# One order of work for five engines, searched again: 1789 operations re-listed, 39 of them on another engine

## The chip, the cores and the metric

The kernel runs on one core of a Trainium2 chip. Five engines work there at the same time, each through its own list of instructions in order: TensorE (PE, matrix products; loading its weights is shown as PEld), VectorE (DVE), ScalarE (ACT), GpSimd (POOL) and SyncE (SP). SP, ACT and POOL also issue DMA transfers. An instruction that needs another engine's result waits at the head of its engine's list, and all that stands behind it on that engine waits too. The metric is the device time of one execution in microseconds; before the change the median of three runs is 204.81 us.

## The reference

Two stages follow each other. The first is block-sparse attention for 4 batches, 8 heads, 768 positions and 64 values per head. Keys and queries are cut in blocks of 32; a query block sees its neighbours, the first and the last block, and three drawn blocks; the first and last query blocks see everything.

```python
scores = scale * np.matmul(q, k.transpose(0, 1, 3, 2))
scores = np.where(mask, scores, -1000000000.0)
scores = scores - np.max(scores, axis=-1, keepdims=True)
attn = np.exp(scores)
attn = attn / (np.sum(attn, axis=-1, keepdims=True) + 1e-09)
return np.matmul(attn, v).astype(np.float32)
```

The heads of one position are put side by side (512 values), and the second stage is a feed-forward net with a gate: a product with `w_in` (512 to 1024), relu, a convolution over three neighbouring positions in each of the 1024 features, a sigmoid of it, and a product with `w_out`.

```python
h = np.maximum(x @ w_in, 0.0)
for k in range(K):
    conv_out += conv_w[k][None, None, :] * hp[:, k:k + S, :]
gate = 1.0 / (1.0 + np.exp(-conv_out))
return (h * gate @ w_out).astype(np.float32)
```

## The kernel before

**The pieces of attention.** Two heads make a pair P, so there are 16 pairs, four for each batch. A pair's keys and queries come in by two ways. Pairs 0 to 4 (`kq_transposes`, line 426) are loaded, transposed by PE (`k_tr`, `q_tr`, lines 470 and 508) and copied by DVE or ACT into a slot (`k_cp`, `q_cp`). Pairs 5 to 15 (`kq_crossbar`, line 546) are loaded by POOL, transposed by a DMA that SP issues (`xb`, line 585) and copied by DVE (`stg_cp`, line 592). The mask sits in 24 extra rows of the same tiles, so that a score product adds it; these rows are made on the first microseconds by DVE and ACT (lines 267 to 363). Values are loaded by POOL and copied (`v_cp`, line 622).

**The unit.** The scores are worked off in 144 units of 128 x 1024 numbers (loop at line 724). A unit is two groups of score products on PE (`s`, line 746), one `exp` on ACT (line 757) from one of two PSUM tiles `st` into one of eight SBUF tiles `pt`, and two groups of four products with the values (`av`, line 779). Since there are two `st` tiles, the scores of unit u+2 wait for the exp of unit u. In this document exps and units are counted from 0, in the order in which they are made.

**The feed-forward part.** The positions are cut in nine segments (line 668): seven of 384 positions, one of 256, one of 128. When the four pairs of a segment are through, DVE divides by the row sums (`rcp`, `norm`, lines 696 and 698), the features are turned by a DMA on SP (`x_xb`, line 707) or by PE with a copy behind it (`x_tr`, `x_cp`, lines 717 and 720), and PE multiplies by `w_in` (`f1`, line 895). Relu (line 903) is an operation of ACT or DVE. For most of the work the convolution is three multiplications and two additions on DVE (`mul`, `add`, lines 946 and 956), then a tanh on ACT (line 998), one more addition and the gate's product on DVE (`g1`, `g2`, lines 1001 and 1006). The last segment's convolution is done on PE (`conv`, line 970). PE multiplies by `w_out` (`f2`, line 825, and line 810 for the last 128 rows), ACT or DVE copies the sum out of PSUM (`ev`), and SP or ACT writes it (`out`).

**What sets the order.** The kernel makes 1789 operation objects and doesn't issue them as it makes them. `put_down` (line 95) walks through the text `ORDER` (line 20) and issues them one by one. Two characters number an operation; where it can run on two engines a letter follows (`A` for ACT, `V` for DVE), and where it takes a buffer a character gives the buffer's number. So the text holds the order of every engine's list, the engine of each operation with a choice, and each buffer. The times given to `op` (`{"DVE": 0.6}`, `lat`, `earliest`, `service`, the priorities) and the lists `deps` and `uses` were read by the search that wrote the text; `put_down` reads none of them. The waits between engines come from the tile framework, which sees which tile each instruction reads and writes.

**The gates of the loads.** POOL issues the loads of K, Q and V in one list. From pair 8 on a `pace` stands ahead of a load (lines 415 to 420): POOL copies one number out of the `pt` tile of a chosen unit, so it waits for that unit's exp. `PACE_U` (line 422) gives the units.

**What is told to be apart.** `apart` (line 868) declares that the relus of the segment of 256 positions and the multiplications and gates of the segment ahead of it touch other columns of the feature tile `hE`, so that the framework puts no wait between them.

Of the kernel before, what the change touches and what calls it, by code (L numbers as in the profile page):

```python
# [20 lines left out]
000x010z020B0407080905060b1e00a1f1c01q11s11801m11t1E21G21H030y0e0c0gV0d0nV0f0A0i0hA0WA30UA0oAr41r5r6r7r8r9rarb  # L21
rcrdrerfrgrhrirjrkrlrmrnrorprqrrrsrtrurvrwrx0Y01210ZA014A0VA13A0mA0XV0jV0+V0lV0t0uryrzrArBrCrDrErFrGrHrIrJrK
15017A16ArLrM4n04o0/14s14t1g11j04p00q10V0p11V1hV11lV1kV4u11dV01iV4x04yrN0rOrPrQ4C14D4z2rRrSrTrUrVrWrXrY4H04I
4E34J44q14r4v4w4Q14R4S54A4B4F4G0s0r1rV14V04W4K1u04X64+14/5071x11vV21yV1zV4L0530544T4U4Y4Z5c15d510E15505e10C1wV
4M01FV24N0F0k5h05i1I0525j21JV35m15n5o31L1561NV575811MV5r05s5f15g5w15x1KV1911n00I5t45y55F05G1bV591S30O0P0Q0R46
1A0470S481O1490T4a1U44b1V4c2404d2634e271TV34f2c14g2e04h2f4i2k24j2m11aV1oV0N1pV5H65k5l5p5q5K15L5M75u5v5z5P05Q
5A05I4O15R05U15V5W15J5a05N610625O5S5T5X5Y6324PV00J5bV5B20D5C5Z35+661675D15EV6416b06c5/0651B160V0K1DV1CV6836d4
0w0v6g16hhq0hr6i56l06m6n6ht1hu6t16uhsV0hvVhO0hQhP6v7hI0hJ6y06zhw1hxhKA6A0hyVhRhS6D16E69hz0hA6F16a1P16e6f6j6I0
6k6J6ohBA1QVhW11RVhT6q0hX6r6K26Q1hF06RhGhC1hD6S3hEAhHVhU6V06W6+11W06p06/6X47056w6x6B73074hL1hM781756hNA796C6G
7a77g06H6L6M6T17h6U6Y1Z17i07l17m6Z717276777q07r7b7n1hYhZi221XV41YVi3i4h+hV06N1i5ia36O1+Vh/ib7d21/V25V4i0ic7ei6  # L30
7s27v17w7c0ii07jio17kid7D07E7x37o7p7t7u7y7z7F4i76s1280292g12h6P7f7I17J7N07G17H7O7A37K5i17P67Biei8i92aV02bVifig
ih2dV02iV17Cijip7S17Tiq7X07Lik7U77Y7M7Q7R831847Vir7Z0851880897Wil8d18e7+8a22jVisV04k2n4l2s34mimV18002lV12tV281
iu18i08j8f38k4ix0iyizV8q18riviwViS4iTiUiV8v08wiA0iBiD1iE8s58x6iCAiFAi+0iW2o22p2qV22rV2u2002v22x2w8A18B7/08F086
878GiG08b8c8g8hiJ1iH8C78H0iXiIA8l8m8t18K18L8S08T8uiK2108yj08n1i/8oj122ViLV23Vj61j28M18U28z8X18Y8D8E8I8J90091
8Z3925j38N8O08ViM1951iP0969769d08WiQiNiOA8+9e8/939i194989j998P2j7iYj8j4iZj98Qj59a3iRVja9bje29f79k1jfjgjhji9n0
9o9p3jE1jbjs09g19s19t9u69h9l9x09yjt9z79mjF9F19q9r9G9v9w9A9K09L9B0jcjdjGjujj9H19M62F2G42C2D02Q2I2H2N2O12R32T2S
2Y2Z22y08222z2J18p8R9c9P19Q9R4jkjljHjIV29C02AV39Djv9I9U09Va019Ja1jN1jOjwA39W0a22jK0jLjMA1jPV0Gk63a50a6aa1jQ19N
abjT0jRk7k8jSVk9jUa75ac3jVA2/30032312Kaf0agak1alah7jZ1j+am1j/A9O9SjW09T9X9Yas0a31ata4a8jXa9ax1ayk31k4ke4kakb0L
kg9Z10H2BVjYVkm0knkf2LV4au6az4aC0aDaE0k00adk1aH1aeaIk2AaiajanaP0aQaJ2jm0jnkh9+ki2MVap2k5Vkcku1aU1aVaR5aW3kjjo
aZ0a+jpao0avawb21b3jy1aAaBaFaGaKaLa/7aqkv2EV32PV4kpkd1kob70b8kqkxaM3kk2+V0aNkwkl9E32U22Vin330jxarit349/b46jqA4  # L40
jzbf1bgb94jAjBbk0kI0aS1blaTaXaYaObh0krbm2jCA1bp1b0bqb1b5kJbu0bvb6ksky2WV02XVktbr5kzkAkBkC1babb0kD373833a3b13f
3c3d3ebw13mbC1bDbc035V1kEkKbH0kFbE3bIbM1bNkLkGV339A1bdkMV036VkO1kPbibJ7bO6kQVbR0bSkR0kSbT4kTVla2lblcldlebW1bj
bXbnbobsbY0kX1c20c3btkU0c71c8c42c95kYkVbxbykWAkZVbz2bAli3cc0cdbF1bGch1cibKl11ce1lfbLl2cp0cj3cqk+0bPbQbUbVbZb+0
cu1ljlklll3Vlmb/1lgc0cr7lnlhloc5l71cvk/l0Alq4cz0c6cacbcfcgcAcw6l40lplrlsltl5l8ckcE1clcFcm3l9VlucB0l6Aly0lzcnlB
lAlC3p3n03q23u3r3s3tcG4cJ0cKcs1ctcxcycClM0cL2lvcR1lG1cDcScW0cT5cHcXcY3cIlNcMcN0lHcUcVc/1d0d40d5lDjDbe03g13hjJ
c1bB3v23wcokHd17lwlxd66cZlIc+lOdc1ddde43iV2lElFd2lP3jVlQV1lJdh0lKA2didj5dm1dnm20m3d3do73E3B3F43J3G3xV3m4V0cO0
cPme1mfmgV3yVdr0d7dsm50m6dw1d8dxdt1m7Vmq1mrmsmtmud913oV23H3T3U33C13Idy03Y3V3W3Q3R23X43443df1mb1dE0dFdG2m80m9mc
dJ1mdAmaAdadKdgdO0dPdL6dQ3mh1mk0mlmidkdT1dUdldpdqdudvmjAd/0e0dzmn1dV4e41e5dA0dHdImoe15e67mpAe90eaeb1mvmy2mmVmz
mG3mImHmJmKmAdB2mBdCmCmO4lS0dMdNdRee1dSefdWdXlTe21e3lY1eg0mLdY3mwmx0mPlUej0eklZl+lVe7l/mDmQdZmRmMmS3DV3mEel2
m0A3e8er1esecew0edehexet6kN3kjr3K03LlR3Z1cQ1lWA0mFn01eieB1eCemn1mN3MV4mTey3eD4mUmV3NVeo0epmW0mXen0mYmZeG0eH  # L50
m+A4n2n3db3+3/V03zlLdDn4V140V3SV4eO1eP3Pd+nf0m1423leq2lX3O3An5ngnc1nd45A0eI5eQ7neAnhVnC0eT0eUeY1eZn90nan61n7
eV1e+0nEnDnbVn8AnFnu1f10f2euevf61f7nl0ezf32nmni1fe0f86nvnGnwnHnxnnVffeAnjeEnkVfj1fkeFeJeKfg3fl4nynzeL1nK2nLeM
nMnIeR1eSeWeXfo0fpno0e/f0ft1fuf4f5fq5f9nr1nsfv7fa0fB0fCnpfhfG1fHfifmfnfrfsfwfxfb2nNnAnJnqVnBntAfcnOfy3nS3fD1
fI0fL0fMfzn+1fN2fT1fUfE1fFo40nTnUnVnWfY0fJfZfKnPfV641eNfdfAf+3nXnQfOn/o5nRg11g2fPfQ0fW0fXf/g90g0g34gao0o6gb5g4
ge1gffRnYnZo7o1o2V2o8A3gg7gj0gkg5om0ong610MooA1gl1op1oqgc1gr1g7orVoK4oMoLoNoOov0gsgt0os1gdowoxAgw0otouAgxgB1gh
gCgioB0gmgnoCgy2oS0go2oDVgpfS3g8o9gqgD6oPgK0oy1ozgLgP1oH0oIgQgu0oAAgM3oE1gvgzgAgEoFgX0gYgR4oJAoGAoToUo+1o/p0p1
oVgFh31gN1gZ5gG3oQgHoWoXog0gOgSohgU0p62h4gI1h80h9gT0oiojp7oYp8oR1p9gVgJApap2h57okA0pq1prhh1g+pz0g/h61pApsApC3
h01ha1pBApbp3oa1h7hbobocodh1pEpDpFhd2pcpdp4oZpt0puhioeA1pvAgW0h2m/hep5pK4pLpw1pxhj0pyAhc0pk0plpmhf1pnhkhlpGpN
p+2p/hm3hnpMq1hgApoA3pHpOpS0pTpIpUpVpJpWpe1pfpgho0phhpApiA4ql0qmqnAqo1qpqi0qz1qAqjpPqqAqB1qkApppjolo3ofqE0qF
qr1qsqu1qvpQqCpRq60q7qDq0pXqtAqw3qG4qxq2q3qypYpZqc1qJ1qKqdqO0qL1qeqHq4qMq5q8q9qNqIqaA3qfqPqQqRqgA4qbqhqSA0qTS  # L60
qU0qVqWqXq+1qYA2qZSq/r0r1r2Ar3A
# [52 lines left out]
def kernel(  # L114
# [118 lines left out]
    o_pad = op("pad_mem", {"DVE": 0.4}, pad, -18, after=[o_amem])  # L233
# [4 lines left out]
    def dma(name, eng, dst, src, prio, deps=(), service=0.3, kind="hw", **kw):  # L238
        occ = {"SP": 0.46, "ACT": 0.1, "POOL": SW}[eng]
        return op(name, {eng: occ}, lambda e: on(e).dma_start(out=dst(), in_=src), prio, deps,  # L240
                  dma=(kind, service), **kw)

    qf, kf = o2s_t[0], [o2s_t[1], o2s_t[2]]
    def first_q(x, e, prio, after):
        return dma("ld_q0", e, lambda: qf[:, 192 * x:192 * x + 192],
                   q[0, x, 0:384].rearrange("(p c) d -> p (c d)", p=128), prio, service=0.38, earliest=1.0, after=after)

    def first_k(x, e, prio, after):
        return dma("ld_k0", e, lambda: kf[x][:, 0:384], k[0, x].rearrange("(p c) d -> p (c d)", p=128), prio,
                   service=0.75, earliest=1.0, after=after)  # L250
# [4 lines left out]
    ld_sb = op("ld_sb", {"SP": 0.46}, lambda e: nc.sync.dma_start(out=sbi, in_=sampled_blocks.bitcast(I32)), -21,  # L255
               after=[k0], lat=1.8)
# [813 lines left out]
```

## Time and profile before

| what | before |
|---|---|
| median of three runs (lowest, highest) | 204.81 us (204.47, 206.22) |
| span of the profiled execution | 202.8 us |
| busy: PE, PEld | 196.8 us (97%), 153.9 us (76%) |
| busy: ACT, DVE, POOL | 189.7 us (94%), 181.8 us (90%), 57.5 us (28%) |
| exps | 144, 1039 ns each |

The profiled execution's own whole time is not among the three runs; the median stands 2.0 us above its span, which is what lies around the first and the last instruction. Busy time counts the engine's own instructions, not those that issue DMAs. Products on PE overlap, so that a busy PE need not be a PE at its best rate. The chain that ended last is the profile's way back from the last instruction: at each step to what released it, or to its forerunner on the same engine.

### The profile page before, as it was taken

How to read it: one execution, taken by the hardware profiler on the slowest of the kernel's cores; microseconds unless marked ns; L12 is line 12 of the kernel's file. 1: busy time of each engine (PE TensorE's matmuls, PEld its weight loads, DVE VectorE, ACT ScalarE, POOL GpSimd, SP SyncE). 2: the span in 40 equal slices, each digit the busy share in tenths (PEclk: the TensorE clock that was granted, in tenths of full speed). 3: DMA queues.
4: the chain of work that ended last, by engine and by line, in shares of the span. 5: the costliest groups of instructions: out<-in, count | busy, mean ns of one | idle time of the engine just before them, and what ended most of it. 6: DMA issues, size and time to landing. Idle time of an engine off the chain costs nothing.

```text
span 202.8 us, 6814 instructions
## 1 busy us (share of the span) xinstructions
PE 196.8 (97%) x2708; PEld 153.9 (76%) x2708; DVE 181.8 (90%) x572; ACT 189.7 (94%) x251; POOL 57.5 (28%) x112
## 2 busy tenths in 40 slices
PE   7899999999999999999999999999999999999993
PEld 7799977986788777877688877876678877876742
DVE  7999989999999979999899988999899968999950
ACT  6999999999999999999999998999999989998842
POOL 8870568630520354202534328400000000000000
PEclk9999999999999999999999999999999999999999
DMA  6999999999998399956869699994321202001515
GB/s 143 177 223 207 182 135 132 167 171 151 155 122 129 61 141 154 213 106 132 133 108 159 82 197 218 135 176 115 124 72 24 41 14 68 13 10 60 204 63 202
DMA packets 53655, 25.96 MB, mean 128 GB/s; under 512 B 39616, under 2 KB 50584, under 8 KB 53624
## 3 DMA queue, kind: packets, MB, share of 16 engines
q0 software_dynamic: 19984, 11.24, 43.7%
q1 hardware_dynamic: 33208, 13.87, 34.6%
q8 instruction: 21, 0.34, 0.7%
q10 hardware_dynamic: 432, 0.43, 0.6%
q14 instruction: 10, 0.08, 0.1%
HBM read 23.08 MB, written 6.29 MB: 145 GB/s over the span
## 4 chain that ended last, share of the span: by engine, by line
PE 78%; ACT 15%; issue 3%; DVE 2%; DMA 1%; ACTq 0%
PE st L746 25%; PE mix L895 18%; PE mix L825 17%; PE av L779 14%; ACT pt L757 11%; DMA o2s<-in_k_dram 1%; DVE e L330 1%; ACT m L998 1%; PE mix L810 1%; PE st L825 1%; PE av L970 1%; ACT nat L328 1%; PE mix L508 1%; ACT hE L915 0%; ACT o2s L328 0%
## 5 line engine op out<-in xcount | busy, mean ns | idle before, releaser
L757 ACT ACTIVATE pt<-st 128x1024 bf16<-128x1024 f32 x144 | 140.6, 1039 | 1.8 <-PE st L746 0.9
L779 PE MATMUL av<-vt,pt 128*128 128x65 bf16 x1152 | 59.9, 193 | 0.2 <-DVE vt L330 0.2
L779 PEld LDWEIGHTS <-pt 128*128 128x128 bf16 x1152 | 52.3, 97 | 9.9 <-issue 0.3
L895 PE MATMUL mix<-xT,winb 128*128 128x384 bf16 (+2 forms) x288 | 53.6, 308 | 0.1
L949 DVE TENSOR_SCALAR m<-hE,cw 128x382 bf16<-128x382 bf16 (+2 forms) x192 | 49.3, 316 | 0.5 <-ACT hE L915 0.2
L825 PE MATMUL mix<-woutb,gT 128*128 128x512 bf16 x176 | 47.1, 379 | 0.3 <-DVE gT L1006 0.3
L746 PE MATMUL st<-o 88*128 88x128 bf16 (+1 forms) x240 | 43.9, 229 | 0.4 <-ACT pt L757 0.3
L746 PE MATMUL st<-o,e 88*128 88x128 bf16 (+1 forms) x228 | 43.4, 233 | 0.0
L746 PE MATMUL st<-e,o 88*128 88x128 bf16 (+1 forms) x224 | 42.3, 234 | 0.2 <-ACT pt L757 0.2
L746 PE MATMUL st<-e 88*128 88x128 bf16 (+1 forms) x208 | 40.9, 239 | 0.1
L746 PEld LDWEIGHTS <-o 88*128 88x128 bf16 x464 | 34.7, 97 | 7.7 <-issue 0.8
L746 PEld LDWEIGHTS <-e 88*128 88x128 bf16 x436 | 33.0, 97 | 7.1 <-issue 0.4
L959 DVE TENSOR_TENSOR m<-m 128x764 bf16<-128x764 bf16 (+2 forms) x64 | 33.5, 532 | 0.4
L895 PEld LDWEIGHTS <-winb 128*128 128x128 bf16 x288 | 24.0, 97 | 8.0 <-issue 0.5
L998 ACT ACTIVATE m<-m 128x764 bf16<-128x764 bf16 (+2 forms) x32 | 26.3, 829 | 0.5 <-DVE m L959 0.3
L825 PEld LDWEIGHTS <-gT 128*128 128x128 bf16 x184 | 15.0, 97 | 9.3 <-DVE gT L1006 0.5
L417 POOL COPY pace<-pt 1x1 bf16<-1x1 bf16 x24 | 6.2, 257 | 49.9 <-ACT pt L757 49.8
L1006 DVE TENSOR_TENSOR gT<-m,hE 128x764 bf16<-128x764 bf16 (+3 forms) x36 | 18.0, 510 | 0.5
L698 DVE TENSOR_TENSOR xtok<-av,rcp 128x384 bf16<-128x384 f32 (+2 forms) x36 | 18.2, 506 | 0.3
L915 ACT ACTIVATE hE<-mix 128x384 bf16<-128x384 f32 (+2 forms) x36 | 17.7, 507 | 0.7 <-PE mix L895 0.5
L240 POOL DMA_DIRECT2D nat<-in_q_dram x23 | 16.8, 733 | 3.2 <-issue 2.5
L917 DVE TENSOR_SCALAR hE<-mix 128x384 bf16<-128x384 f32 x28 | 15.3, 549 | 2.6 <-PE mix L895 2.2
(84 smaller groups left out, 157.4 us busy)
## 6 DMA issues: line engine op xcount, KB each, us to landing
out_dram<-o2s SPq DMA_DIRECT2D x23, 256.0 KB
vn<-in_v_dram POOLq DMA_DIRECT2D x16, 192.0 KB, 5.0
nat<-in_k_dram POOLq DMA_DIRECT2D x15, 192.0 KB, 4.7
nat<-in_q_dram POOLq DMA_DIRECT2D x7, 192.0 KB, 5.2
winb<-in_moe_w_in_dram POOLq DMA_DIRECT2D x2, 512.0 KB, 9.5
woutb<-in_moe_w_out_dram POOLq DMA_DIRECT2D x4, 256.0 KB, 8.2
nat<-in_q_dram POOLq DMA_DIRECT2D x8, 96.0 KB, 4.5
nq<-in_q_dram POOLq DMA_DIRECT2D x5, 96.0 KB, 5.2
```

Source lines behind the costliest of these rows:

```text
L240: return op(name, {eng: occ}, lambda e: on(e).dma_start(out=dst(), in_=src), prio, deps, dma=(kind, service), **kw)
L698: nm = op("norm", {"DVE": t_dps(128 * C)}, lambda e: nc.vector.tensor_tensor(out=xtok_t[xk.index][:, 0:C].rearrange("p c h d -> p h c d"), ...
L746: nc.tensor.matmul(out=st[:, 128 * x:128 * (x + n_)], lhsT=QK[kc % 2][s][0:88, 1, hh, kc // 2, :], rhs=QK[par][s][0:88, 0, hh, idx:idx + n ...
L757: nc.scalar.activation(out=pt_t[ptb.index], in_=st_t[stb.index], func=AF.Exp, bias=0.0, scale=0.125)
L779: nc.tensor.matmul(out=o[:, off:off + 65], lhsT=pt_t[ptb.index][:, 128 * x:128 * x + 128], rhs=V_t[vslot_b[P].index][:, hh, kc, 0:65], sta ...
L825: nc.tensor.matmul(out=acc(), lhsT=gT_t[gb.index][:, ffc, 128 * t:128 * t + 128], rhs=woutb[:, ffc, :], start=(ffc == 0), stop=(ffc == NFF ...
L895: nc.tensor.matmul(out=mix_t[hb.index][:, w1 * y:w1 * y + w1], lhsT=winb[:, fc, 128 * ffc:128 * ffc + 128], rhs=xT_t[xt_buf[n].index][:, f ...
L915: i = nc.scalar.activation(out=dst, in_=src, func=AF.Relu, bias=0.0, scale=0.5)
L949: i = nc.vector.tensor_scalar(out=m_t[cb.index][:, x, y, 0:w], in0=hE_t[heb.index][:, f0 + y, t0 + x:t0 + x + w], scalar1=cw[:, x, f0 + y: ...
L959: nc.vector.tensor_tensor(out=m[:, a_, :, 0:w], in0=m[:, a_, :, 0:w], in1=m[:, b_, :, 0:w], op=ALU.add)
L998: th = [op("tanh", {"ACT": t_act(2 * w) + 0.04}, lambda e, cb=cb, w=w: nc.scalar.activation(out=m_t[cb.index][:, 0, :, 0:w], in_=m_t[cb.in ...
L1006: i = nc.vector.tensor_tensor(out=gT_t[gtb.index][:, f0:f0 + 2, t0:t1], in0=m_t[cb.index][:, 0, :, 0:w], in1=hE_t[heb.index][:, f0:f0 + 2, ...
```

## The change

The operations stay the same ones. Three things differ in what runs.

1. **The order.** All 41 lines of `ORDER` are replaced. On average an operation moves by 3.4 places in PE's list, 3.6 in DVE's, 1.6 in ACT's, 2.9 in SP's and 3.9 in POOL's. 39 operations change between ACT and DVE: ACT gives up three copies that bring feed-forward sums out of PSUM (it loses five `ev` and gets two), one `v_cp`, and five small copies of the first microseconds; it gets one `q_cp` of pair 4, two relus more than before (12 for 10), and of the first microseconds one `cast_k` and two `k_cp`. In all ACT has 249 operations in its list instead of 252, DVE 447 instead of 444. The exps of units 29 and 30 change places.
2. **The gates of the last loads.** `PACE_U` is replaced by 24 numbers, `PACES`. The last query loads (pair 15) wait for exp 106 instead of exp 101, the last value load stands behind them; most other loads are let go earlier or as before. The keys of pair 13 wait for exp 0 by the list and those of pair 10 for exp 10, and their `pace` copies stand behind exps 23 and 25 in the order, so that two of the eight `pt` tiles are kept until then.
3. **What is told to be apart.** `apart` now covers all segments, and relus of two engines on one feature tile are told to be apart as well.

The numbers for the search change in many places (an issue on ACT's queue 0.45 instead of 0.1, durations taken from traces, times of the first loads). They don't act on what runs.

```diff
@@ ORDER
-000x010z020B0407080905060b1e00a1f1c01q11s11801m11t1E21G21H030y0e0c0gV0d0nV0f0A0i0hA0WA30UA0oAr41r5r6r7r8r9rarb
...
-qU0qVqWqXq+1qYA2qZSq/r0r1r2Ar3A
+0a040500010z0B020br41070603r5r61e0r7r80c08r9rarbrc0erd091frerfrN00drgrhrirj1c0rkrl0gV0hArmrnrorprq1q10nVrr0WA1
...
+qZSr2Ar3A
@@ costs that the search reads
-        occ = {"SP": 0.46, "ACT": 0.1, "POOL": SW}[eng]
+        occ = {"SP": 0.46, "ACT": 0.45, "POOL": SW}[eng]
@@ gates
-    def PACE_U(P):
-        b, j = divmod(P, 4)
-        return 36 * (b - 1) + ((12, 17, 22, 28) if b == 1 else (4, 12, 20, 27))[j]
+    PACES = (43, 43, 31, 29, 44, 59, 10, 39, 41, 38, 53, 57, 43, 53, 66, 0, 46, 96, 66, 78, 82, 64, 106, 98)
...
-        pc = pace(PACE_U(P), due - 14) if b > 1 else None
+        pc = pace(PACES[3 * (P - 8)], due - 14) if b > 1 else None
...
-            pq = pace(PACE_U(P) + 2, due - 12)
+            pq = pace(PACES[3 * (P - 8) + 1], due - 12)
...
-                pv = pace(PACE_U(P) + 4, due - 9)
+                pv = pace(PACES[3 * (P - 8) + 2], due - 9)
@@ apart
-    def apart(n, pr, x, inst):
-        if n in (NSEG - 3, NSEG - 2):
-            for other in side.get((pr, 1 - x), []):
+    def apart(n, pr, x, inst, e):
+
+        for other, by in side.get((n, pr, 1 - x), []):
+            if by != e:
                 tc.declare_no_dep(inst.ins, other.ins, reason="other columns of the feature tile")
-            side.setdefault((pr, x), []).append(inst)
+        side.setdefault((n, pr, x), []).append((inst, e))
+
+    wrote = {}
@@ relu
-                if n == NSEG - 2:
-                    apart(n, fg, 0, i)
+                for m in range(n):
+                    if SEGS[m][0] == SEGS[n][0]:
+                        for y in range(FB * fg // 2, (FB * fg + FB - 1) // 2 + 1):
+                            apart(m, y, 0, i, e)
+                for y in range(FB):
+                    for other, by in wrote.get((SEGS[n][0], FB * fg + y), []):
+                        if by != e:
+                            tc.declare_no_dep(i.ins, other.ins, reason="other columns of the feature tile")
+                    wrote.setdefault((SEGS[n][0], FB * fg + y), []).append((i, e))
```

More of the change, by code (lines that the diff above doesn't have):

```diff
@@ L26 @@
[L26 to L35, printed above, removed]
```

169 lines of the change are left out of this document (88 added, 81 removed).

## The prediction

> **What bounds the kernel now.** First the page's span and busy times, then the engines' busy time by stretches, because an average over the whole span hides which of two nearly full engines leads.
>
> ```profile
> span 202.8 us, 6814 instructions
> ...
> PE 196.8 (97%) x2708; PEld 153.9 (76%) x2708; DVE 181.8 (90%) x572; ACT 189.7 (94%) x251; POOL 57.5 (28%) x112
> ```
>
> ```profile
> 7.50:67.00 59.50, 58.40 (x926) 49.39 (x924) 56.05 (x168) 59.01 (x71) 25.53 (x50) 1.00 1.19 162
> 67.00:170.00 103.00, 103.00 (x1399) 78.48 (x1399) 95.13 (x279) 100.87 (x126) 25.51 (x48) 1.00 0.74 119
> 170.00:196.00 26.00, 25.86 (x302) 18.55 (x300) 24.72 (x95) 21.82 (x39) 0.00 (x0) 1.00 0.21 73
> ```
>
> The columns are the stretch, its length, then the busy time of PE, PEld, DVE, ACT and POOL. Up to 67 us ACT is idle for 59.50 - 59.01 = 0.49 us and PE for 1.10 us; from 67 to 170 us PE is never idle and ACT is, for 2.13 us. So the lead passes from ACT to PE at about 67 us. The chain of the work that ended last shows the place, and then the end:
>
> ```profile
> 65.89 1.06 ACT pt L757
> ...
> 66.99 0.60 PE st L746 x6
> 67.59 0.86 PE mix L825 x4
> 68.46 0.12 PE av L779 x4
> ```
>
> ```profile
> 188.66 0.45 PE mix L825 x2
> 189.10 0.02 issue
> 189.12 0.59 ACT o2s L328
> ...
> 189.76 0.83 PE mix L895 x12
> ...
> 196.51 1.29 PE st L825 x6
> 197.81 1.76 PE mix L810 x16
> ```
>
> Exp 54 (counted along ACT's list) ends at 65.89 + 1.06 = 66.95, the scores that need its PSUM tile start at 66.99, and behind them PE has work until 197.81 + 1.76 = 199.57, with one wait, of at most 189.76 - 189.11 = 0.65 us. The rest, 199.57 to 202.8, is the last copy out of PSUM and the last write. So the time is: when ACT gets through exp 54 (or whichever exp PE waits for last), plus PE's work behind it, which no order shortens, plus 3.2 us, plus the 2.0 us that the median of the runs stands above the span. The sum is made on the span.
>
> **The change part by part.** Start. ACT's list up to its first exp, then PE's and DVE's:
>
> ```profile
> 3.64 0.77 ACT L328 CAST nat<-o2s 128x384 bf16<-128x384 f32 x2
> 4.43 0.51 ACT L328 COPY o<-o 24x384 bf16<-24x384 bf16 x1
> 4.96 0.47 ACT L328 COPY e<-mix 64x384 bf16<-64x384 bf16 x1
> 5.45 0.26 ACT L328 COPY o<-mix 64x128 bf16<-64x128 bf16 x1
> 5.74 0.35 ACT L328 CAST nat<-o2s 128x192 bf16<-128x192 f32 x1
> 6.12 0.37 ACT L328 COPY e<-mix 64x256 bf16<-64x256 bf16 x1
> ...
> 7.58 4.66 ACT L757 ACTIVATE pt<-st 128x1024 bf16<-128x1024 f32 x5
> ```
>
> ```profile
> 8.09 0.40 PE L508 MATMUL mix<-ident,nat 128*128 128x128 bf16 x4
> 8.65 0.22 PE L746 MATMUL st<-e,o 88*128 88x128 bf16 x1 [0.16 <-ACT pt L757]
> ```
>
> ```profile
> 4.61 0.85 DVE L314 TENSOR_SCALAR e<-may 24x144 bf16<-24x144 bf16 x4
> ...
> 6.42 0.36 DVE L330 COPY o<-mix 64x384 bf16<-64x384 bf16 x1
> ```
>
> In the new list ACT does behind the first two casts, from 4.43 on: a cast of 128x384 (0.51, by the copy of as many columns at 4.43), the two query copies (0.26 and 0.37), two key copies (0.47 each) and the second query cast (0.35). That is 2.43, and 0.02 or 0.03 between each two, so 6.98 instead of 7.58: **0.60 earlier**. What the first exp needs is there: DVE copies the keys behind the mask rows, 4.61 + 0.85 + 0.36, so about 5.85, and two groups of scores take at most 0.60 (the row at 66.99), so 6.45. But the gain doesn't reach the third exp whole. Its scores stand in both lists behind the transposes of pair 1, whose second half runs from 8.09 to 8.49 as its load comes in; now exp 0's end releases them at 8.65. With exp 0 ending at about 8.0 they start at 8.49 at the earliest and are done by 9.1, where exp 2 can begin. Now it begins at 7.58 + 2 x 0.93 = 9.44 (five exps in 4.66): **0.30** are left of the gain, which I take. The ends are 0.60 and 0: DVE has nine small operations from 5.85 on to the last copy that unit 2 needs, and at 0.36 each that is 9.1, with scores behind it 9.4.
>
> ACT's load up to exp 54. Four relus leave this stretch and four come; one copy of 64x512 (`q_cp` of pair 4) comes. That form has no row on ACT: it lies between 0.47 (64x384, the row at 4.96) and 0.59 (the 128x512 copy at 189.12); I take 0.53. Of the 0.49 us of idle time I let 0.20 come back, with 0 and 0.49 as ends. Together ACT gets to exp 54 at -0.30 - 0.20 + 0.53 = **+0.03**.
>
> PE's work behind that place. In the new list one pair of `f2` products (half of 0.86, so 0.43) comes ahead of the scores of unit 56 and one group of `av` (0.12) goes behind them: 0.31 less is left. At the scores of unit 62, which wait for exp 60, it is the other way: one pair of `f2` more is left, 0.43.
>
> ```profile
> 71.97 2.84 ACT L757 ACTIVATE pt<-st 128x1024 bf16<-128x1024 f32 x3
> ```
>
> ```profile
> 74.48 0.22 PE L746 MATMUL st<-o 88*128 88x128 bf16 x1
> ```
>
> The three exps are 59 to 61, at distances of 0.91, so exp 60 ends at 73.90; the scores of unit 62 start at 74.48. Sums: by exp 54, 66.99 + 0.03 + (199.57 - 66.99) - 0.31 = 199.29. By exp 60, 73.90 + 0.03 + 0.04 + (199.57 - 74.48) + 0.43 = 199.49. The later one decides: **PE ends 0.08 earlier**. With the good ends (0.60, 0.49, 0.47) it is 198.80, 0.77 earlier; without any gain and 0.59, 200.05, 0.48 later.
>
> The order of the last 10 us on PE is nearly the same; the copy for the first half of the last rows goes from ACT to DVE, beside the last products, and is not on the path. The wait at 189.1 stays, or goes: 0 to -0.65.
>
> The `pt` tiles kept for two `pace` copies leave seven and then six to the exps up to exp 25. PE's list has the `av` group that frees a tile ahead of the scores each time there, so that costs nothing; if it does, it is the kind of wait that ACT has once now:
>
> ```profile
> 123.29 1.02 ACT L757 ACTIVATE pt<-st 128x1024 bf16<-128x1024 f32 x1 [0.19 <-PE av L779]
> ```
>
> In the old order three exps have the freeing `av` behind their own scores on PE, in the new order five, two of them (52 and 55) ahead of the crossing: 2 x 0.19 = 0.38 at most. The new declarations of `apart` take away waits; the list of waits before the change has no relu that waits for a multiplication, so that alone is worth nothing.
>
> Loads. They are let go earlier except the last ones:
>
> ```profile
> 128.29 1.95 ACT L757 ACTIVATE pt<-st 128x1024 bf16<-128x1024 f32 x2
> ```
>
> ```profile
> 134.31 1.55 SPq L585 DMA_TRANSPOSE stg<-nat  x1
> ...
> 139.69 1.20 SPq L707 DMA_TRANSPOSE xT<-xtok  x1
> ```
>
> ```profile
> 147.44 1.30 PE L895 MATMUL mix<-xT,winb 128*128 128x384 bf16 x7
> ```
>
> ```profile
> nat<-in_q_dram POOLq DMA_DIRECT2D x8, 96.0 KB, 4.5
> ```
>
> Those two exps are 105 and 106. So the last queries go at about 130.3 in three issues on POOL, of which I allow 2 us for all, and land by about 130.3 + 2 + 4.5 = 137. Now their transpose is issued at 134.31, and feature transposes stand behind it on SP, the last of that segment at 139.69; the segment's first product runs at 147.44. Nearly 3 us later, the last feature transpose is issued at 142.4 and still has 5 us to that product: it costs nothing.
>
> **Forecast:** span 202.8 - 0.1 = 202.7, with the 2.0 outside it **204.7 us, no change**. Its own ends: 0.77 + 0.65 earlier (203.4) to 0.48 + 0.38 later (205.7).
>
> **The rivals.** *Slower: DVE leads at the end.* Between the first division of the segment of 256 positions and the last gate DVE is all but full:
>
> ```profile
> 171.34 0.18 DVE L696 RECIPROCAL rcp<-av 128x4 f32<-128x4 f32 x1
> 171.66 0.56 DVE L917 TENSOR_SCALAR hE<-mix 128x384 bf16<-128x384 f32 x1
> ```
>
> ```profile
> 176.91 0.99 DVE L949 TENSOR_SCALAR m<-hE,cw 128x382 bf16<-128x382 bf16 x4
> ```
>
> ```profile
> 179.69 1.01 DVE L959 TENSOR_TENSOR m<-m 128x764 bf16<-128x764 bf16 x2
> ```
>
> ```profile
> 194.57 0.83 DVE L1006 TENSOR_TENSOR gT<-m,hE 128x512 bf16<-128x512 bf16 x3
> ```
>
> The last gate ends at 195.40, and from 170 to 196 the idle time is 26.00 - 24.72 = 1.28, of which 0.60 lies behind that gate. The new list moves two `mul` operations (four instructions, 0.99) and two `add` (1.01) behind that division and one relu (0.56) away: 1.44 more. On PE the `av` that releases the division comes two groups of scores (0.60 at most) and two pairs of `f1` (1.30 for seven products at 147.44, so 0.37 a pair) sooner, some 1.2 us. So DVE is 0.2 late, which the gates' lead hides: the last gate ends 1.1 us ahead of the products from 196.51 on. If DVE can't use the earlier start, because tanh and relu reach it no sooner, it is 1.44 late, and up to 0.68 more if as many idle moments come on top. It decides from 1.1 us on where PE's list is as now, and sooner where the new list has products of the tile ahead earlier. Price 0.3 to 2.1: 205.0 to 206.8, likeliest 205.7.
>
> *Slower: the last loads.* A 192 KB query load took 8.8 us between issue and landing when many went at once:
>
> ```profile
> nat<-in_q_dram POOLq DMA_DIRECT2D x1, 192.0 KB, 8.8
> ```
>
> With that the last queries land at 141.1; the feature transposes behind them move by 6.8 us, the last one is issued at 146.5, and with 1.2 for itself and as much to land PE waits 1.5 us for it, 2 to 3 if the other small writes on SP pile up: 206.2 to 207.7. It decides from a landing of some 7 us on.
>
> *Faster: everything gives.* The good ends above, 0.77 + 0.65 earlier, give 203.4; ACT's whole head start with PE's order as good as its list allows, 1 us more, 202.4. For it: both engines show idle time up to 67 us. Against it: the sums by exp 60.
>
> *Faster: PE has room.* PEld is busy for 78.48 of the 103.00 us from 67 to 170, against 49.39 of 59.50 before. Were the weight loads as dense later as earlier (83% against 76%), 103 us would be 94.6, and the time 196. Against it: the pieces of the chain stand end to end, and `f2` at 0.86 for four products is the same everywhere; the lower share comes with longer products per load. The Trainium skill (Perfetto Trace Analysis, Identifying the Most-Contended Engine) says that PE's matmul busy share is not a good measure of how near it is to its best, and that the share of weight loads is better; by it PE at 76% has headroom. The trace doesn't bear that out for an order of the same products.
>
> That the change doesn't do what it says is no case here: the lists run as written.
>
> **How the numbers follow.** Forecast 0.53; DVE at the end 0.21, a third of it over 1%; last loads 0.15, two thirds over; everything gives 0.09, half over; PE has room 0.02. A measurement of this kernel can tell about 1% (2.05 us) from no change. Slower by over 1%: 0.07 + 0.10 = 0.17. Faster: 0.04 + 0.02 = 0.06. Within: 0.77. The range is 203.3 to 207.0: it leaves out the last case, part of the one ahead of it and the worst of the loads.
>
> **What would show it.** The first exp at about 7.0 and the third at about 9.1; exp 54 ending within 0.5 of 66.95; PE without idle time from 67 to 189; DVE's last gate within 1 us of 195.4 and no wait of `f2` for a gate; the last `xb` issued at about 137. The prediction is wrong if PE's work behind the crossing is shorter or longer than 132 us, if exps early in the list wait for DVE's copies, or if PE shows waits for gates or loads behind 67 us.

## The result, and the profile after

| what | before | after |
|---|---|---|
| median of four runs each, one more of before than in the table above (lowest, highest) | 205.30 us (204.47, 206.22) | 208.03 us (207.44, 208.62) |
| ratio of the times, 95% interval | 1 | 1.0131 (1.0081 to 1.0180) |
| span of the profiled execution | 202.8 us | 205.7 us |
| PE's last product ends at | 199.57 | 202.45 |

The changed kernel is 1.3% slower. The forecast of 204.7 us and no change was wrong, and 208.03 lies above the range (203.3 to 207.0). The profiled execution after took 207.44 us as a whole, so 1.74 us lie around its span. In all executions with a span on record it is 1.72 to 1.84 us; the 2.0 us used so far compared a median with the span of one of the faster executions. In some kernels below one or two executions were longer than the rest whatever the list (in `l2_new_end` 210.62 us at a granted clock of 0.992, the others 206.31 to 207.30), and all times and ratios below leave these out.

First the busy times on the page of the changed kernel:

```profile
PE 196.5 (96%) x2689; PEld 153.7 (75%) x2708; DVE 183.4 (89%) x575; ACT 189.2 (92%) x248; POOL 59.0 (29%) x112
```

The busy times of PE, DVE and ACT are as before to 1%, so none of the three has much more to do. PE ends 2.88 us later (202.45 against 199.57) because it waits longer. Where, the busy time by stretches shows (length, then PE, PEld, DVE, ACT and POOL, then the granted clock, the DMA engines' share and GB/s; the changed kernel, the same stretches as in the prediction):

```profile
7.50:67.00 59.50, 56.62 (x876) 47.52 (x880) 54.26 (x164) 57.06 (x68) 28.86 (x58) 1.00 1.12 159
67.00:170.00 103.00, 102.14 (x1400) 78.05 (x1411) 95.35 (x279) 100.36 (x125) 23.41 (x40) 1.00 0.73 116
170.00:196.00 26.00, 25.64 (x316) 19.36 (x319) 24.99 (x92) 22.93 (x40) 0.00 (x0) 1.00 0.28 93
```

Up to 67 us PE is idle for 2.88 us (1.10 before) and ACT for 2.44 (0.49 before). Behind it PE's idle time grows by 0.86 and by 0.22. Most of that is no waiting: the page has 2689 product records against 2708 weight loads, and before it had 2708 of both, so 19 records are missing and leave small gaps. Two runs further below have the old list from 67 to 170 us and miss 11 and 12 records there (`e4_old_order`, `h1_new_start`); they show 0.96 and 0.73 us of idle time in that stretch (0.28 of the 0.96 is a listed wait), where the kernel before, with no record missing, has none. The loss lies mainly ahead of 67 us, where both engines that could lead wait more.

The list of PE's waits names what came last (total, times, longest, in us). `e` and `o` are the tiles that hold keys, queries and mask rows, `xtok` the divided features and `xT` the turned ones; line numbers differ a little between the kernels (the scores are line 746 before and 743 after). Before, and then after, without the first wait of 1.1 that both have:

```profile
PE av L508 <- ACT nat L328: 0.5, 1, 0.5
PE st L746 <- ACT pt L757: 0.4, 2, 0.3
PE mix L825 <- DVE gT L1006: 0.3, 1, 0.3
PE av L779 <- DVE vt L330: 0.2, 1, 0.2
```

```profile
PE st L743 <- ACT pt L754: 1.0, 3, 0.6
PE st L743 <- DVE o L329: 0.8, 1, 0.8
PE mix L895 <- DMA xT<-xtok: 0.8, 1, 0.8
PE st L743 <- DMA e<-e: 0.5, 1, 0.5
PE av L776 <- DVE xtok L695: 0.2, 1, 0.2
```

The listed waits grew from 2.5 to 4.4 us; the other microsecond of the 2.88 lies in pieces too small for the list. Four kinds are new: a wait for DVE's small copies at the start (`o`, until 7.54 us), one for feature transposes (`xT<-xtok`), one for the mask rows that a DMA copies into a further slot (`e<-e`), one for a division (`xtok`). No listed wait lies behind 56 us. The chain of the work that ended last has the two transfers at full length:

```profile
41.31 4.33 DMA e<-e
...
45.69 0.70 PE st L743 x6
...
51.19 4.59 DMA xT<-xtok
...
55.82 0.99 PE mix L895 x5
```

Both were issued by SP. SP's list before, and then after:

```profile
8.03 1.48 SPq L361 DMA_DIRECT2D o<-o  x2
9.56 0.71 SPq L361 DMA_DIRECT2D e<-e  x1
...
35.13 1.29 SPq L707 DMA_TRANSPOSE xT<-xtok  x1
```

```profile
39.97 1.29 SPq L704 DMA_TRANSPOSE xT<-xtok  x1
41.31 0.75 SPq L360 DMA_DIRECT2D e<-e  x1
42.10 0.72 SPq L360 DMA_DIRECT2D o<-o  x1
```

The feature transpose of segment 1's first pair is issued 4.84 us later, and the row copies, which were issued by 10.3 us before, stand behind it. What it waits for is the division, `norm`; DVE's list before, and after:

```profile
34.02 0.20 DVE L696 RECIPROCAL rcp<-av 128x6 f32<-128x6 f32 x1
...
34.56 0.55 DVE L698 TENSOR_TENSOR xtok<-av,rcp 128x384 bf16<-128x384 f32 x1
```

```profile
35.46 0.20 DVE L693 RECIPROCAL rcp<-av 128x6 f32<-128x6 f32 x1
...
39.39 0.55 DVE L695 TENSOR_TENSOR xtok<-av,rcp 128x384 bf16<-128x384 f32 x1
```

The reciprocal is 1.44 us later, the product with it 4.83: the new list puts nine operations (a copy, a relu and pieces of gates) between the two. The transpose that waits for it stands at the head of SP's list, and all that is behind it there waits too. This became the first theory.

### The profile page after: what moved, and what is told of

Its sections match the earlier page's. It is cut to its first block, busy times and chain, and to the rows that moved or that the text cites. A ratio compares the mean times of both kernels' runs of the same rounds, so it can differ in the third digit from the quotient of the medians.

```text
span 205.7 us, 6810 instructions
## 1 busy us (share of the span) xinstructions
PE 196.5 (96%) x2689; PEld 153.7 (75%) x2708; DVE 183.4 (89%) x575; ACT 189.2 (92%) x248; POOL 59.0 (29%) x112
## 4 chain that ended last, share of the span: by engine, by line
PE 74%; DVE 12%; ACT 5%; DMA 4%; issue 2%; SPq 0%; ACTq 0%
PE st L743 23%; PE mix L895 17%; PE mix L822 17%; PE av L776 12%; ACT pt L754 4%; DVE m L956 3%; DVE o L329 2%; DMA xT<-xtok 2%; DMA e<-e 2%; DVE e L329 2%; PE st L1032 2%; DVE m L965 1%; DVE hE L917 1%; PE mix L807 1%; PE st L822 1%
## 5 line engine op out<-in xcount | busy, mean ns | idle before, releaser
L776 PE MATMUL av<-vt,pt 128*128 128x65 bf16 x1152 | 59.3, 193 | 0.3 <-DVE xtok L695 0.2
L895 PE MATMUL mix<-xT,winb 128*128 128x384 bf16 (+2 forms) x288 | 54.3, 308 | 0.9 <-DMA xT<-xtok 0.8
L822 PE MATMUL mix<-woutb,gT 128*128 128x512 bf16 x157 | 44.2, 379 | 0.8
L743 PE MATMUL st<-e 88*128 88x128 bf16 (+1 forms) x208 | 41.6, 239 | 0.6 <-DMA e<-e 0.5
L895 PEld LDWEIGHTS <-winb 128*128 128x128 bf16 x288 | 23.0, 97 | 7.4 <-issue 1.5
L1004 ACT ACTIVATE m<-m 128x764 bf16<-128x764 bf16 (+2 forms) x32 | 26.9, 842 | 0.2 <-DVE m L965 0.2
L416 POOL COPY pace<-pt 1x1 bf16<-1x1 bf16 x24 | 7.9, 328 | 64.2 <-ACT pt L754 64.0
L915 ACT ACTIVATE hE<-mix 128x384 bf16<-128x384 f32 (+2 forms) x38 | 18.7, 502 | 1.9 <-PE mix L895 1.7
L917 DVE TENSOR_SCALAR hE<-mix 128x384 bf16<-128x384 f32 x26 | 14.4, 553 | 5.8 <-PE mix L895 5.2
## 6 DMA issues: line engine op xcount, KB each, us to landing
winb<-in_moe_w_in_dram POOLq DMA_DIRECT2D x2, 512.0 KB, 10.3
```

Of the source, the lines that this page charges most:

```text
L743: nc.tensor.matmul(out=st[:, 128 * x:128 * (x + n_)], lhsT=QK[kc % 2][s][0:88, 1, hh, kc // 2, :], rhs=QK[par][s][0:88, 0, hh, idx:idx + n ...
L776: nc.tensor.matmul(out=o[:, off:off + 65], lhsT=pt_t[ptb.index][:, 128 * x:128 * x + 128], rhs=V_t[vslot_b[P].index][:, hh, kc, 0:65], sta ...
L822: nc.tensor.matmul(out=acc(), lhsT=gT_t[gb.index][:, ffc, 128 * t:128 * t + 128], rhs=woutb[:, ffc, :], start=(ffc == 0), stop=(ffc == NFF ...
L895: nc.tensor.matmul(out=mix_t[hb.index][:, w1 * y:w1 * y + w1], lhsT=winb[:, fc, 128 * ffc:128 * ffc + 128], rhs=xT_t[xt_buf[n].index][:, f ...
L915: i = nc.scalar.activation(out=dst, in_=src, func=AF.Relu, bias=0.0, scale=0.5)
L1004: th = [op("tanh", {"ACT": t_act(2 * w) + 0.04}, lambda e, cb=cb, w=w: nc.scalar.activation(out=m_t[cb.index][:, 0, :, 0:w], in_=m_t[cb.in ...
```

## The experiments

All times are compared with runs of the kernel before on the same chip, taken beside them. Not all kernels ran on one chip, so two rows are compared by their ratios. Several kernels join the new and the old list: up to a named exp the operations of the one list, then all that are left in the order of the other, with buffers numbered anew where a number was taken.

| kernel | time, us | ratio to before, 95% interval |
|---|---|---|
| changed kernel | 208.03 | 1.0131 (1.0081, 1.0180) |
| division early (`e1_norm_first`) | 207.06 | 1.0078 (1.0042, 1.0115) |
| mask rows early (`e2_rows_early`) | 206.89 | 1.0079 (1.0044, 1.0114) |
| both early (`e3_both`) | 206.92 | 1.0090 (1.0061, 1.0119) |
| old list, new declarations (`e4_old_order`) | 205.26 | 1.0020 (0.9992, 1.0048) |
| new to exp 18, then old (`h1_new_start`) | 205.82 | 1.0031 (1.0005, 1.0057) |
| new to exp 56, then old (`h3_old_tail`) | 208.50 | 1.0158 (1.0109, 1.0207) |
| old to exp 112, then new (`l2_new_end`) | 206.68 | 1.0080 (1.0049, 1.0111) |
| DVE's new order alone, exps 18 to 56 (`g3_dve_sp`) | 211.21 | 1.0274 (1.0231, 1.0317) |
| both early, no tile kept (`k2_free_tiles`) | 206.76 | 1.0100 (1.0078, 1.0121) |
| the same with the old start (`k3_old_start`) | 207.13 | 1.0122 (1.0093, 1.0151) |
| both early, old engine choices (`k4_old_engines`) | 214.38 | 1.0438 (1.0396, 1.0480) |

### The division and the mask rows

```diff
@@ e1: DVE's list
 rcp (410)
+norm (411)
 v_cp, mul, g1, add, relu, add, mul, mul, g2
-norm (411)
@@ e2: SP's list
+m_dma (31), m_dma (32)
 x_xb (412)
-m_dma (31), m_dma (32)
@@ e3: both
```

> The new list with one operation moved: the `norm` of the first head pair of segment 1 (op 411) stands directly behind its `rcp` (410) on DVE instead of ten operations later. Theory A, a late division holds the head of SP's queue: in the profile after, its feature transpose was issued at 39.97 (35.13 before) and everything behind it on SP, two mask-row copies and ten transposes, came later too; PE then waited 0.70 us at 45.7 for mask rows, 0.95 at 55.8 for feature transposes and 0.33 at 40.0 for the same division. With the division at about 36 these 2.0 us go: span 203.7, time 206.0. Theory B, the exps' and scores' interleaving in the new list is worse from 28 us on whatever the transposes do: other waits take the place of these, span 205.2 to 205.7, time 207.5 to 208.0. Theory C, DVE is simply too full from 30 to 67 us: half comes back, span 204.7.

> The new list with two operations moved: the copies of the mask rows for the fourth and fifth slot (ops 31 and 32) stand ahead of the feature transpose of segment 1 on SP, as they do before, and the division stays late. Theory A: the wait of 0.70 at 45.7 goes, and the queue behind is 1.6 us shorter, so that the wait of 0.95 at 55.8 goes as well; the wait of 0.33 at 40.0 stays: span 204.0, time 206.4. Theory B: 207.5 to 208.0. Theory C (DVE too full): the first wait goes and comes back as waits for DVE: 207.3 to 208.0.

> Both moves at once. Theory A: the same 2.0 us as with the division alone, since either move empties SP's queue in time: span 203.7, time 206.0; what is then left over the kernel before is 0.5 us from the start of the list and 0.5 us of small waits behind 67 us. Theory B: 207.5 to 208.0. If mask rows and division each cost something that the other move alone doesn't give back, this one is the fastest of the three, by 0.3 or more.

Each of the three came out at 206.9 to 207.1, about 1 us below the changed kernel (0.4 to 0.5% by the ratios; the single intervals overlap with that of the changed kernel, the three agree). Either move alone gives what both give. Theory A had said 206.0 to 206.4, so its mechanism was there and its price was not. A part of that price was a misreading: the expectations put the three waits at 2.0 us, and the list has 0.53, 0.78 and 0.16 for them, 1.5 in all. SP's list with the division early:

```profile
36.49 1.30 SPq L704 DMA_TRANSPOSE xT<-xtok  x1
37.84 0.75 SPq L360 DMA_DIRECT2D e<-e  x1
```

The transpose is back at 36.49, and PE's list of waits in this run has neither `xT<-xtok` nor `e<-e`. What it has instead:

```profile
PE st L743 <- ACT pt L754: 1.4, 5, 0.6
PE st L743 <- DVE o L329: 1.1, 2, 0.8
```

Waits of scores for exps are now 1.4 us in five places (1.0 in three in the changed kernel), those for DVE's copies 1.1 in two (0.8 in one); the new one, 0.36 at 67.1 us, is for queries that DVE copies. PE's idle time up to 67 us is 2.48, 2.50 and 2.27 us in the three runs, against 2.88. So some of what was removed came back as other waits. By the times about half came back, which is theory C's size; that the new waits had been covered by the old ones is the likely reading, and no run shows it apart.

### The declarations alone

```diff
-ORDER, PACES: new
+ORDER, PACES: as before
```

> The changed program with the old list and the old gates of the loads: only the new declarations of `apart` are left of the change. As predicted these are worth nothing: 205.3, within 0.5 of the kernel before. Rival: that the declarations change the waits on other instructions and cost something by themselves: 206.5 to 208.

205.26 against 204.73, ratio 1.0020 with 1 inside the interval: worth nothing that these runs can tell, as forecast. The execution of this kernel that was profiled took 206.48 us, the longest of its twelve (204.50 the shortest), and shows by chance what a late transpose does in the old list. SP's key and query transposes in the kernel before, in this execution, and then its chain and a row of DVE:

```profile
36.53 7.51 SPq L585 DMA_TRANSPOSE stg<-nat  x4
```

```profile
36.62 8.44 SPq L582 DMA_TRANSPOSE stg<-nat  x4
```

```profile
41.73 10.88 DMA stg<-nat
...
53.74 0.69 DVE o2s L329
```

```profile
52.70 0.55 DVE L329 COPY e<-stg 64x1536 bf16<-64x1536 bf16 x1 [1.57 <-DMA stg<-nat]
```

The four took SP 0.93 us longer, and the last of them landed at 52.61. DVE's copy out of its stage had waited 1.57 us for it, the copy out of PSUM behind it (`o2s`) came late, and PE's next product waited 1.4 us, until 54.48, for the PSUM tile `mix`. So the place around 55 us has next to no slack in the old list either.

### Which stretch

```diff
-ORDER: new throughout
+h1: new up to exp 18, old behind
+h3: new up to exp 56, old behind
+l2: old up to exp 112, new behind
```

> The new list up to exp 18, the rest of the operations in the old list's order, with the gates of each part. Theory D, the loss comes between exp 18 and exp 56 (25 to 68 us) and neither from the start nor from the end of the list: as the kernel before, 204.9 to 205.2. Theory E, the start costs, since PE's idle time up to 16 us is 1.0 us longer in the run with both moves than in the kernel before (3.41 against 2.38): 205.5 to 205.9.

> The new list up to exp 56, the old one behind it. Theory D: as the changed kernel, 207.3 to 207.6, since the loss lies ahead of the cut. Theory F, the new list's end costs too (the profile after has 0.6 us of PE waits behind 70 us, of which some are small waits for exps at 98, 106 and 118 us): 0.4 to 0.6 less, 206.9 to 207.2.

> The old list up to exp 112 (138 us), with the old loads and gates, and the new one behind it: the last 60 us alone, with eight changed engine choices, the two `mul` pairs, two `add` and an output copy that the new list moves behind the first division of the segment of 256 positions, and the copy of the last rows moved to DVE. The prediction's forecast for this stretch: no change, 204.9 (0 to -0.65). Its rival, DVE leads at the end: 205.4 to 206.8.

The run with the new start alone is 0.3% (0.6 us) slower, theory E's lower half. Its profiled execution doesn't show the start to be at fault. Exp 16 begins at 22.17 there, 0.28 us ahead of the kernel before, and the next loss stands at the joint behind exp 18:

```profile
25.65 0.29 PE L776 MATMUL av<-vt,pt 128*128 128x65 bf16 x4 [0.49 <-ACT pt L754]
```

Exp 54 then begins 0.06 us late. This execution, at 204.83, was one of the fastest of the twelve, so the 0.6 us of the median are not found in it. The sign that theory E went by, 1.0 us more idle time of PE up to 16 us, was too large as well: by the busy times it is 2.55 us in the run with both moves and 2.01 before.

With the old list put back behind exp 56, all of the loss stays (1.0158), so it is made ahead of that place. Theory F, that the end costs as well, went by small gaps behind 70 us, of which the list of waits names none and which are of the size that missing records leave. In this run nothing came back, though a wait of 0.41 us for an exp at 73.09, just behind the joint, could hide what theory F has. PE's busy time in the run with the old end:

```profile
7.50:67.00 59.50, 54.97 (x854) 1.00 1.09 155
```

That is 4.53 us of idle time up to 67 us, before the old list takes over; the changed kernel, with the same list, had 2.88 in its profiled execution, so the loss also varies from execution to execution. The last run has the new end by itself, and came out 1.6 us slower, inside what the rival at the end would give (205.4 to 206.8). Its profile says otherwise; PE's waits and a stretch:

```profile
PE st L743 <- ACT pt L754: 1.5, 3, 0.9
...
PE mix L895 <- ACT o2s L327: 1.1, 2, 0.9
```

```profile
170.00:196.00 26.00, 25.81 (x318) 19.18 (x316) 24.99 (x93) 22.89 (x40) 0.00 (x0) 1.00 0.27 89
```

The two waits of 0.9 each lie between 140 and 149 us, where the lists are joined. From 150 us on PE is never idle up to 170, and for 0.19 up to 196 (0.14 before). DVE does 24.99 us of work in the last stretch (24.72 before) and PE doesn't wait for it. So by PE's waits the end, with its eight changed engine choices, neither costs nor gains.

Seven further runs join the lists in other ways or vary the loads. They were spoiled: in each, waits at a joint or for the loads outweigh the rest.

```diff
@@ h2: old to exp 18, then new with both early        h4: old to exp 56, then new; gates of the first part at exp 55
@@ g1, g2: the same, with POOL's old list and gates    g4: new throughout, both early, POOL's old list and gates
@@ k1, l1: as h4, with POOL's new list; in l1 no tile is kept for a gate
```

> The old list up to exp 18, the rest in the new list's order, with the division of segment 1 early and the mask rows early: so all that the two moves gave, and the old start. Theory D: as the run with both moves, 206.7 to 206.9. Theory E: 1.0 us less, 205.9.

> The old list up to exp 56, the new one behind it (gates that name an exp of the first part name exp 55 or the last one ahead of them instead). This is the part of the prediction by exp 60 taken alone: PE 0.1 earlier, 204.8. Theory D: as the kernel before, 204.6 to 205.2. Theory F: 205.3 to 205.5. The rivals of the prediction at the end of the list, DVE's last gates or the last loads late, would give 205.7 and more.

> The old list up to exp 56 and the new one behind it on PE, ACT, DVE and SP; GpSimd keeps the old kernel's whole list of loads and its gates, so that no load comes late at the seam. This takes alone the prediction's sum by exp 60: 0.1 earlier than the kernel before, 204.9. Theory D (the loss lies between exp 18 and exp 56): 204.7 to 205.3. Theory F (the end costs by itself): 205.4 to 205.6. The prediction's rival of DVE's last gates: 205.7 and more.

> The old list up to exp 18 and the new one behind it, with the division of segment 1 and the mask rows early, and GpSimd's list and gates as before. Theory D with the 0.6 us that the start alone has cost: 206.3 (the run with both moves, 206.9, less 0.6). If the new gates of the loads, too, cost something, less: 205.8. If the start is the whole rest of the loss: 205.0.

> The whole new list with the division of segment 1 and the mask rows early, and GpSimd's list of loads and gates as before the change. As predicted the release points of the loads cost nothing: as the run with both moves, 206.9. Rival: that loads let go earlier run beside SP's transposes and slow them, or that kept `pt` tiles stop exps: 206.2 to 206.4.

> The old list up to exp 56 and the new one behind it on PE, ACT, DVE and SP, now with the new list of loads and the new gates on GpSimd throughout, since the old loads proved too late for the new list. The prediction's sum by exp 60 alone: 204.9. Theory D (the loss lies ahead of exp 56): 204.7 to 205.4. Theory F (the end costs by itself, an exp's wait for a gate at 105.7 among it): 205.5 to 205.9. The rival of DVE's last gates: 205.7 and more.

> The old list up to exp 56 and the new one behind it, with the new list of loads, and gates and `pt` tiles as in the run that keeps no tile long (in the earlier attempt at this, exps waited 14 us for tiles that gates kept). Theory D (the loss lies ahead of exp 56): 204.7 to 205.5. Theory F (the end costs): 205.6 to 206. More than 206.5 means that the new list's end can't stand on the old beginning, and says nothing on either.

They took 214.96 (h2), 219.4 (h4), 223.25 (g1), 224.31 (g2), 223.77 (g4), 224.14 (k1) and 208.82 us (l1), and say nothing on the end. They do show that loads and gates belong to a list. The run with the new list and the old loads, its chain:

```profile
124.99 2.53 DMA nat<-in_q_dram
127.53 2.81 DMA stg<-nat
...
132.61 7.14 DMA xT<-xtok
```

The new list needs its loads earlier. Where they come by the old gates, stage copies on DVE and transposes on SP wait at the head of their lists, feature transposes stand behind them, and PE waits, 3.4, 3.0 and 2.4 us at the longest. Behind these waits the clock that is granted to PE is lower, and its products take longer too. The end of that chain, columns as above:

```profile
130.00:145.00 15.00, 9.94 (x57) 6.01 (x58) 6.06 (x12) 4.06 (x6) 5.48 (x10) 0.54 1.19 167
```

The clock is 0.54 there, and PE is busy for 202.8 us in this run, 6 us more than before the change with the same products. Waits and clock together make some 16 us more than the run with both moves. And with tiles kept for gates, exps stop; ACT's longest wait in one of these runs (h2; in k1 such waits sum up to 14.0 us):

```profile
ACT pt L754 <- POOL pace L416: 7.0, 1, 7.0
```

### Kept tiles, engine choices, DVE's order

```diff
@@ k2, k3 (k3 on the old list up to exp 18)
-PACES = (43, 43, 31, 29, 44, 59, 10, 39, 41, 38, 53, 57, 43, 53, 66, 0, 46, 96, 66, 78, 82, 64, 106, 98)
+PACES = (43, 43, 31, 29, 44, 59, 24, 39, 60, 38, 53, 76, 43, 53, 80, 21, 46, 96, 66, 78, 96, 79, 106, 98)
@@ k4
-the new list's engine letters
+the old list's engine letters, in the new order
@@ g3
-DVE's list between exps 18 and 56: old
+DVE's list between exps 18 and 56: new
```

> The new list with the division and the mask rows early, and seven gates moved to a later exp, so that none keeps a `pt` tile for long (gate 10 becomes 24, gate 0 becomes 21, 66 becomes 80 and so on); the `pt` tiles go round in turn over all eight. Theory H, a tile kept for a gate stops an exp: in the run with both moves an exp waited 0.57 for a gate's copy at 34.0 and another 0.36 at 105.7; without these 0.6 to 0.9 less, 206.0 to 206.3. If the waits are covered by what PE has to do: 206.9.

> As the one before, with the old list up to exp 18. With the 0.6 us that the new start alone has cost: 0.6 below the one before, 205.5 by theory H, 206.3 without. If both and the two moves are the whole loss, it is as the kernel before, 205.0 to 205.3.

> The new list with the division and the mask rows early, and all 39 changed engine choices as before (the order of the operations is kept). The prediction took the changed choices for worth nothing but the copy that comes to ACT: as the run with both moves, 206.9. Rival: the choices cost, since ACT has one relu and one copy more between exp 20 and exp 36, where PE waits 1.5 us longer for exps: 206.0 to 206.3. Or the new list lives on its choices: 207.5 and more.

> The old list and the old engine choices; only the order of DVE's operations between exp 18 and exp 56 is the new list's (the division of segment 1 behind ten other operations), PE's and ACT's order is the old one throughout. Theory A (a late division holds SP's queue): as in the profile after, PE waits 0.3 for the division and up to 0.95 for feature transposes, 206.0 to 206.3. Theory B (the loss comes from how PE's and ACT's lists interleave): 205.0 to 205.3.

Kept tiles do stop exps. In the changed kernel, and then in the run with both moves:

```profile
105.75 1.02 ACT L754 ACTIVATE pt<-st 128x1024 bf16<-128x1024 f32 x1 [0.36 <-POOL pace L416]
```

```profile
34.03 1.02 ACT L754 ACTIVATE pt<-st 128x1024 bf16<-128x1024 f32 x1 [0.57 <-POOL pace L416]
```

But with no tile kept for long the time stayed (ratio 1.0100 against 1.0090). The two waits are gone there, and another of 0.46 at 61.8 us has come, so these waits look covered, and theory H finds no support. Neither did the old start give 0.6 us back under the new middle (207.13); but that run has the new list of loads throughout, and PE waits 0.85 us at 20.84 for a query load, as the two other runs with an old start and that list of loads do (0.74 in k1, 0.77 in l1). So it tells little of the start.

Taking the engine choices back doesn't help: with the old ones the new order loses another 7 us (214.38), with waits of products for relus on DVE, and of scores for exps, as the largest:

```profile
PE st L743 <- ACT pt L754: 2.2, 7, 0.7
PE mix L895 <- DVE hE L917: 2.2, 3, 1.1
```

And DVE's new order under the old lists of PE and ACT costs 5.6 us, some five times what theory A had for it; PE's waits there:

```profile
PE av L776 <- DVE xtok L695: 1.6, 1, 1.6
...
PE mix L714 <- DVE xT L329: 0.8, 1, 0.8
PE st L743 <- DVE o L329: 0.8, 1, 0.8
PE mix L822 <- DVE o L329: 0.7, 1, 0.7
PE mix L822 <- DVE gT L1012: 0.7, 1, 0.7
```

PE waits directly for five of DVE's results, none of them by way of SP. DVE's order fits the order of the other lists it was made with; of the parts tried here only the start and the end could be carried into the other list at a cost of under 1%.

## Why the prediction was wrong

**The frame held in part.** Its sum was: when ACT is through exp 54, PE's work behind it, 3.2 us, and what lies around the span. In the changed kernel:

```profile
68.21 1.94 ACT L754 ACTIVATE pt<-st 128x1024 bf16<-128x1024 f32 x2
```

```profile
69.22 0.38 PE L822 MATMUL mix<-woutb,gT 128*128 128x512 bf16 x1
...
69.56 0.22 PE L743 MATMUL st<-o 88*128 88x128 bf16 x1
```

The first of these two exps is exp 54; it ends at 69.24, 2.3 us later than before. The scores of unit 56 begin at 69.56, 2.57 later, and PE needs another 132.89 to its end (132.58 before). So 2.57 of the 2.88 us are there by then. But PE doesn't wait for exp 54: it has the `f2` product ahead of these scores, and its last listed wait ended at 55.82, for feature transposes. In this execution the place from which PE works on without a listed wait was thus set by SP's transposes and not by ACT.

**The term that failed** is the step "ACT's load up to exp 54", and in it "Of the 0.49 us of idle time I let 0.20 come back, with 0 and 0.49 as ends". ACT's idle time didn't shrink, it grew to 2.44, by 1.95. (The copy that was taken for 0.53 took 0.57.) The ends of the term were both gains, although the list of this stretch was new on all engines; nothing had excluded a loss. The prediction counted ACT's own work and looked for waits in SP's list only at the last loads, from 128 us on. The chain from DVE's late division by way of SP's list to PE's scores and products, around 35 to 56 us, was in none of its steps and rivals, though the lists showed both moves. The two moves put back take away 0.4 to 0.5% of the 1.3%, so this chain is a part of what failed; what makes the rest of the added idle time stays open. A small slip in the sum changes nothing: with the good ends it gives 198.84, 0.73 earlier, and not 198.80.

**Start.** The first exp begins at 6.91 (forecast 6.98, before 7.58). The next ones:

```profile
8.29 20.18 ACT L754 ACTIVATE pt<-st 128x1024 bf16<-128x1024 f32 x21 [0.36 <-PE st L743]
```

The third begins at 9.45; before, it began at 9.40 (the prediction reckoned 9.44). Of the gain nothing is left, not 0.30. That was the lower end of the step, and its reason was named: DVE's small copies come too late (the wait of 0.8 for `o` above). It isn't so in every execution, though. Other runs with the same list up to there have the third exp at 9.07 (`h1_new_start`, `e2_rows_early`), as forecast, or at 9.62 (`h3_old_tail`), with waits of 0.30, 0.49 and 0.70 for `o`.

**PE's work behind the crossing** was to be 0.31 shorter by exp 54, and is 0.31 longer, though the `f2` product stands ahead of the scores as the prediction has it. No listed wait lies behind that place, so the difference of 0.6 us is in pieces too small for the list, and its cause stays open. The condition in the text, 132 us, holds to 1 us.

**Rivals.** DVE doesn't lead at the end: its last gate ends at 198.99, 0.7 us nearer to PE's end than before, and PE doesn't wait for it. PE's last wait is as before, 0.14 us for ACT's copy of a feed-forward sum (0.59 at 192.00, at 189.12 before). The last loads' transpose was issued at 140.12, not 137, and the segment's first product didn't wait for it. So the loads did cost nothing there, but only with the list that belongs to them. That rival allowed 1.2 us for a feature transpose to land, which no row had; the one issued at 51.19 in the changed kernel took 4.59 from its issue. PE having room: its weight loads are busy for 75% of the span (76% before), and in no profiled run did PE end earlier than in the kernel before. The Trainium skill (Perfetto Trace Analysis, Identifying the Most-Contended Engine) takes the busy share of weight loads, and not that of products, for how near PE is to its best. By that PE would have room; no order of the same products tried here found any.

**Kept tiles and declarations** were forecast at nothing and were worth nothing in time that these runs can tell, though exps did wait for gates: in the changed kernel once, 0.36 us at 105.75, and with both moves also at 34.03, where the text had excluded it.

**What stays open.** Of the 1.3%, 0.4 to 0.5% hang on the late division and the row copies. The start makes at most 0.3%, and its profile doesn't show that much. The rest, half or more, arises between exps 18 and 56 and was not tied to any one move: with both moves put back the profile shows scores waiting for exps between 36 and 44 us and for copied queries at 67, and no run took these away. The diff lowers the search's cost of a transpose on SP from 1.4 and 1.35 to 1.25, while SP's four key and query transposes took 7.5 and 8.4 us in two executions of the old list. In the changed kernel four took 5.55. That the search saw no price in holding SP's list for this reason is an argument, and no run showed it. Nor did any run show whether the loads, let go earlier, slow these transposes, since the run with the old loads was spoiled.

## What to carry to other kernels

When the order of several in-order lists is exchanged, look in every list, SP's and POOL's too, for an instruction whose releaser moved later, and count what stands behind it; in the stretch here, where two engines were 98 and 99% busy before (58.40 and 59.01 of 59.50 us), such waits were not made up. Give a term for idle time a loss as its end, not only a gain, when the lists of all engines are new. A list, its engine choices and its release points belong together: lists joined from two can be slower than either (k1 by 9.7% against the old one), so a joined list says something only where its profile shows no wait at the joint. And a profile is one execution: the same start had its third exp at 9.07 in one run and at 9.62 in another.

## What was not expected of the hardware

A transpose that SP issues held SP for 1.2 us in some places and for up to 3.3 in others: the four that took 7.51 us took 1.22, 1.24, 1.83 and 2.93, and the four that took 8.44 us in another execution of the same list took 1.34, 1.36, 2.11 and 3.34. The last of these landed 10.88 us behind its issue. The kernel before ran from 204.16 to 206.84 us in 22 executions beside the first experiments; the one longer execution of the old list that has a profile lost time behind these transposes. A small transfer among them was no faster: the copy of 24 mask rows issued at 41.31 in the changed kernel took 4.33 us to its landing. And where PE had waited for several microseconds, its granted clock was about half for a while (0.54 from 130 to 145 us in `g4_old_loads`, 1.00 from 80 to 130).
